# Two PSUM pools, single banks for the MLP, a later w1 load and an earlier first gate in a convolution and MLP block

## The chip, the cores and the metric

The kernel runs on one core of one Trainium2 chip. The metric is the device time of one execution in microseconds; the median of several runs is given, and beside it one profiled execution with its own time.

## The reference, cut to what matters

```python
def _A_ref(q, k, v, shift_k, ssm_k, ssm_D):            # S = 2048 tokens, D = 512
    k_shift = ...                                        # 4-tap causal shift filter of k
    kv = k_shift * v
    y = irfft(rfft(kv padded to 2S) * rfft(ssm_k padded to 2S))[:S]
    y = y + kv * ssm_D
    return q * y

def _B_ref(x, w1, w2):                                   # w1: 512 x 1376, w2: 1376 x 512
    return relu(x @ w1) @ w2

x = A_q
h = x + _A_ref(layernorm(x), A_k, A_v, A_shift_k, A_ssm_k, A_ssm_D)
out = h + _B_ref(layernorm(h), B_w1, B_w2)
```

The input and the output are bf16. The FFT stands for a causal convolution over 2048 tokens, of each of the 512 channels with its own filter.

## The kernel before

The instructions of each engine run in the order in which the code records them; the framework adds the semaphore waits. There is no planner that reorders anything. So the order on TensorE (PE), VectorE (DVE), ScalarE (ACT), GpSimd (POOL) and the DMA queue of SyncE (SP) is written out by hand in the source.

The work goes through these stages:

- **Filter and input, first stage (15 to 44 us).** `to_rows` (L278, L279) transposes the filter `sk` through PSUM into `kfl`. The loop over `u` in 0 to 7 then runs `s1(u)` (the first stage of the filter's transform, for one group of channels, with four "spike" matmuls at L293 that add `ssm_D` from `drow`) and `tap(u)` (the shift filter as matmuls at L329, times v at L332). The trigonometric tables are made in a scratch tile between them (`turns2`, L147 and L148; `sines2`, L142).
- **Second stage (44 to 72 us).** `second_k` finishes the filter's transform (L345, evicted at L266 or L268), `to_rows` brings the product `vT` into rows `xfl`, and `stage1_pairs` makes the first stage of the input's transform. In between, `column_means` (L365) forms the column means of w1 on TensorE, and `center` takes them off w1 on GpSimd: this is the second layer norm's mean, folded into w1.
- **Product (72 to 100 us).** `product(kp)` for 16 values of kp: second stage of the input, times the filter's transform.
- **Inverse (97 to 124 us).** 16 turns. Turn i has matmuls into `pi` (L486), a 32x32 transpose on VectorE (`inv_turn`, L491) and a rounding copy, on ScalarE for even i and GpSimd for odd i (`rounded`, L499 and L497). `last(q, d)` (L523) closes the inverse transform for tokens of quarter q and channel half d into `pz`. `last(0, 0)` needs blocks 0 to 7, `last(0, 1)` blocks 8 to 15.
- **Gate.** `gate(q, d)` multiplies `pz` by the normed input `qln` (L534), adds the input (L535) and sends the result `hp` through a transposing DMA into `hT` on SP's queue (L537). `ln1_norm` makes `qln`: on ScalarE for q = 0 (L513), on VectorE otherwise (L515). `norm1(q)` is statistics (L393, L395, and L397 and L398 on GpSimd) plus `ln1_norm`; `norm2(q)` is the statistics of `hp`.
- **MLP.** For each of the four sequence parts `sc` of 512 tokens, `mlp1(sc)` makes h1T = relu(w1^T hT) in 11 chunks of the 1376 columns (matmuls at L572, Relu on ScalarE at L608), and `mlp2(sc)` makes four token tiles (matmuls at L618, 11 in a group), each scaled and added to `hp` on VectorE (`o`, L623, two instructions a tile) and sent out (L627). For the first part `begin()` runs the half of four chunks that only needs `hT` of d = 0, ahead of the other half.

PSUM is one pool `ps` of four tiles, each of two banks of 512 f32, and `bank2(name)` takes the next tile in turn, whatever it is for. In `mlp1` two chunks fill the two banks of a tile, and one Relu of 128x1024 reads both. In `mlp2` two token tiles share a tile, and `o` reads one bank at a time.

The weights w1 are loaded by `load_w1()`: four DMAs of 344 KB on SP's queue (L125), into the same memory slot (tag "w") that the scratch tile held. So they wait until nothing reads the scratch tile any more. It is called after `sines2(1, 1, ...)` at u = 2. w2 is loaded by ScalarE's queue after the first transposes of the MLP (L595, L597).

The order of the MLP's pieces at the end:

```python
norm1(1)
mlp1(0)
norm2(0)
last(1, 0)
gate(1, 0, mp)
last(1, 1)
gate(1, 1, mp)
norm1(2)
mlp2(0)
last(2, 0)
...
```

Of the kernel before, what the change touches and what calls it, by code (L numbers as in the profile page):

```python
# [11 lines left out]
F32 = mybir.dt.float32  # L12
# [43 lines left out]
def kernel(  # L56
# [29 lines left out]
    tabp = pl.push("tabp", side="right")  # L86
    rows = pl.push("rows", side="right")
    early = pl.push("early", side="right")
    psum = pl.push("ps", bufs=4, space=PSUM)


    sk = rows.tile([P, DC, S], BF16, tag="r", name="sk")
    nc.sync.dma_start(out=sk[:], in_=A_ssm_k.rearrange("(c p) t -> p c t", p=P))
    wsh = consts.tile([P, DC, KS], BF16, name="wsh")
    nc.scalar.dma_start(out=wsh[:], in_=A_shift_k.rearrange("(r p) j -> p r j", p=P))
    drow = consts.tile([P, 64], BF16, name="drow")
    nc.gpsimd.memset(drow[:], 0.0)
# [17 lines left out]


    w1 = None
    scratch = w1p.tile([P, 2, 16, 64], I32, tag="w", name="scratch")
# [39 lines left out]
    r2 = scratch[:, 0]  # L158
# [49 lines left out]
    nc.gpsimd.memset(ones[:], 1.0 / D)  # L208

    def turns2(i, b):  # L210
        ta = scratch[:, 1]
        _turns(ta, r2, n2c[:], 8192, o2[:, i, b:b + 1])
        return ta

# [52 lines left out]
        else:  # L267
            nc.vector.tensor_copy(out=o, in_=i)  # L268

    def bank2(name):  # L270
        return psum.tile([P, 2, 512], F32, tag="ps", name=name)


    def to_rows(src, q, fl):
# [127 lines left out]
    for u in range(8):  # L402
        s1(u)
        if u == 1:
            sines2(1, 0, turns2(1, 0))
        if u == 2:
            sines2(1, 1, turns2(1, 1))
            load_w1()
            negated(2)
            negated(3)  # L410
        if u == 4:
            inverse_tables()
        tap(u)
    pl.pop("early")
    xfl = rows.tile([P, 64, 2, 64], BF16, tag="r", name="xfl")

# [90 lines left out]
    def ln1_norm(q, pool, tiles=range(4)):  # L507
        if 0 in tiles:
            qn[q] = pool.tile([P, 4, D], BF16, tag="qln", name="qln", bufs=2 if q else 1)
        for i in tiles:  # L510
            t = 4 * q + i
            if q == 0:
                nc.scalar.activation(out=qn[q][:, i, :], in_=xh[q][:, i, :], func=ACT.Identity, scale=rstd1[:, t, :], bias=nmr[:, i:i + 1])  # L513
            else:
                nc.vector.tensor_scalar(out=qn[q][:, i, :], in0=xh[q][:, i, :], scalar1=mv1[:, t, 0:1],  # L515
                                        scalar2=rstd1[:, t, :], op0=ALU.subtract, op1=ALU.mult)

    def last(q, d):
        pz = bank2("pz")[:].rearrange("p b (i c) -> p (b i) c", c=256)
        pzs[q, d] = pz  # L520
        for i in range(4):
            for t in range(2):
                nc.tensor.matmul(out=pz[:, i, :], lhsT=tf[:, 4 * q + i, t:t + 2].rearrange("p t a n -> p (t a n)"),  # L523
                                 rhs=a1x[:, d, 16 * t + 4 * q + i, :], start=(t == 0), stop=(t == 1))

    def gate(q, d, pool, parts=(slice(0, 4),)):
        if d == 0:
            hp[q] = pool.tile([P, 2, 4, 256], BF16, tag="hp", name="hp", bufs=3 if q else 1)
            hT[q] = pool.tile([P, 2, 4, 2, P], BF16, tag="hT", name="hT", bufs=2 if q else 1)
        part = lambda t: t.rearrange("p i (r d g) -> p i r d g", r=DC, d=2)[:, :, :, d]  # L530
        h = hp[q][:, d]
        for ts in parts:
            hr = h[:, ts].rearrange("p i (r g) -> p i r g", r=DC)
            nc.vector.tensor_tensor(out=hr, in0=pzs[q, d][:, ts].rearrange("p i (r g) -> p i r g", r=DC), in1=part(qn[q][:, ts]), op=ALU.mult)  # L534
            nc.vector.tensor_tensor(out=hr, in0=hr, in1=part(xh[q][:, ts]), op=ALU.add)  # L535
        if (q, d) != (0, 1):
            nc.sync.dma_start_transpose(out=hT[q][:, d].rearrange("p i r t -> p (i r) t"), in_=h.rearrange("p i c -> p (i c)"))  # L537

    blocks = []
    spots = [(i // 8, 32 * (i % 8)) for i in range(16)]  # L540
    tiles = [bank2("pi") for _ in range(2)]
    for b in range(2):
        for i in range(2):
            inv_half(tiles[i], *spots[i], b)
    for i in range(16):
        if i >= 2:
            tiles.append(bank2("pi"))
            for b in range(2):
                inv_half(tiles[i], *spots[i], b)
        blocks.append(inv_turn(tiles[i], *spots[i]))  # L550
        if i < 14:
            rounded("AP"[i % 2], blocks[i])
        if i in (4, 6):
            ln1_norm(0, late, range(i - 4, i - 2))
        if i == 10:
            last(0, 0)
        if i == 11:
            gate(0, 0, late)

    for i in (14, 15):  # L560
# [8 lines left out]
    def first(sc, ps1, fc, cs):  # L569
        fsz = min(P, DFF - fc * P)  # L570
        for c in cs:
            nc.tensor.matmul(out=ps1[:fsz, fc % 2, :].rearrange("p (i t) -> p i t", i=4), lhsT=w1[:, c, fc * P:fc * P + fsz],  # L572
                             rhs=hT[sc][:, c // 2, :, c % 2, :], start=(c == 0), stop=(c == DC - 1))
# [11 lines left out]
    pst = bank2("pst")[:].bitcast(BF16)[:, 0, :].rearrange("p (i t) -> p i t", t=P)  # L585
    for i in range(8):
        nc.tensor.transpose(out=pst[:, i, :], in_=hp[0][:, 1, i // 2, P * (i % 2):P * (i % 2) + P], identity=ident[:])
        if i % 4 == 3:
            nc.scalar.copy(out=hT[0][:, 1].rearrange("p i r t -> p (i r) t")[:, i - 3:i + 1], in_=pst[:, i - 3:i + 1])
    pl.pop("mid")  # L590
    pl.pop("a1kp")
    mp = pl.push("mp", side="right")
# [5 lines left out]
    def mlp1(sc):  # L598
        h1T = mp.tile([P, NFC, 512], BF16, tag="h1T", name="h1T", bufs=2)
        h1s[sc] = h1T  # L600
        for f0 in range(0, NFC, 2):
            fcs = range(f0, min(f0 + 2, NFC))
            early = sc == 0 and f0 // 2 < len(begun)
            ps1 = begun[f0 // 2] if early else bank2("ps1m")
            for fc in fcs:
                first(sc, ps1, fc, (2, 3) if early else range(DC))
            fsz = min(P, DFF - f0 * P)
            nc.scalar.activation(out=h1T[:fsz, f0:f0 + len(fcs), :], in_=ps1[:fsz, 0:len(fcs), :], func=ACT.Relu)  # L608

    def mlp2(sc):  # L610
        h1T = h1s[sc]
        for j in range(2):
            ps2 = bank2("ps2m")
            for i in range(2 * j, 2 * j + 2):
                t = 4 * sc + i
                for fc in range(NFC):
                    ksz = min(P, DFF - fc * P)
                    nc.tensor.matmul(out=ps2[:, i % 2, :], lhsT=h1T[:ksz, fc, i * P:(i + 1) * P], rhs=w2[:ksz, fc, :],  # L618
                                     start=(fc == 0), stop=(fc == NFC - 1))
                o = mp.tile([P, D], BF16, tag="o", name="o", bufs=4)  # L620
                for d in range(2):
                    half = lambda a: a.rearrange("p (r d g) -> p d r g", r=DC, d=2)[:, d]
                    nc.vector.scalar_tensor_tensor(out=half(o[:]), in0=half(ps2[:, i % 2, :]), scalar=rstd2[:, t, :],  # L623
                                                   in1=hp[sc][:, d, i, :].rearrange("p (r g) -> p r g", r=DC),
                                                   op0=ALU.mult, op1=ALU.add)
# [36 lines left out]
    mlp2(3)  # L662
    pl.close_all()

# [29 lines left out]
```

## Time and profile before

| what | value |
|---|---|
| three runs | 241.17 us median, 238.05 to 243.74 |
| the profiled execution | 238.82 us, with a span of 237.0 us from its first to its last instruction |
| TensorE busy | 180.9 us, 76% of the span |
| VectorE busy | 150.1 us, 63% |
| ScalarE busy | 95.3 us, 40% |
| GpSimd busy | 92.1 us, 39% |
| chain that ended last, by engine | PE 52%, DVE 19%, issue 9%, POOL 8%, DMA 5%, ACT 4% |
| mean granted TensorE clock | 0.949 |

The profile gives times in microseconds from the start of the span and durations of one instruction in nanoseconds. PE is the matmul part of TensorE, PEld its weight loads, L572 is line 572 of the kernel. A matmul's end is modelled, so consecutive matmuls overlap in the records. "Issue" is time in which an engine waited for nothing that the profile shows. The granted clock is the share of full clock that TensorE had; it changes between 0.50 and 1.00.

### The profile page before, as it was taken

Reading aid. Unit: us, or ns where it says so; the run is one execution under the profiler, and the core shown is the slowest. Engines: PE = TensorE matmul, PEld = TensorE weight load, DVE = VectorE, ACT = ScalarE, POOL = GpSimd, SP = SyncE. Lnnn points to the kernel's source line nnn. Section 1 sums busy time; section 2 is a strip of 40 time slices with the busy share of each in tenths; the row PEclk is TensorE's granted clock in tenths of the full one; section 3 lists DMA queues with packets and bytes.
Section 4 is the critical chain, followed back from the end, with each engine's and each line's share of the span. In section 5 each row is a group of like instructions: output and inputs, shape, how many; then the busy total and the mean of one; then the engine's idle time right before and its main releaser. Section 6 shows DMA issues by size and latency. Waiting matters only on the chain.

```text
span 237.0 us, 4368 instructions
## 1 busy us (share of the span) xinstructions
PE 180.9 (76%) x1804; PEld 112.5 (47%) x1816; DVE 150.1 (63%) x225; ACT 95.3 (40%) x95; POOL 92.1 (39%) x111
## 2 busy tenths in 40 slices
PE   0489776998986777696947990989909899889883
PEld 0475443687765667474624450344503445334331
DVE  4777984497966999999877767246371372343121
ACT  3214853457799343179772620005400044006300
POOL 7889980008931999858650222002020020002000
PEclk9999999799999999999967996799976999999999
DMA  6999994000000000094020613013021130320011
GB/s 210 280 234 182 188 218 98 3 4 0 3 3 3 1 0 3 0 239 118 0 44 6 232 21 71 22 46 66 0 44 25 46 66 0 66 47 22 0 44 44
DMA packets 31331, 16.00 MB, mean 67 GB/s; under 512 B 26224, under 2 KB 29648, under 8 KB 31312
## 3 DMA queue, kind: packets, MB, share of 16 engines
q1 hardware_dynamic: 28976, 14.05, 27.9%
q10 hardware_dynamic: 2336, 1.68, 2.5%
q8 instruction: 14, 0.23, 0.4%
q14 instruction: 5, 0.04, 0.1%
HBM read 7.54 MB, written 2.10 MB: 41 GB/s over the span
## 4 chain that ended last, share of the span: by engine, by line
PE 52%; DVE 19%; issue 9%; POOL 8%; DMA 5%; ACT 4%; DVEq 0%; SPq 0%; POOLq 0%
PE ps1m L572 16%; PE ps2m L618 13%; POOL a1k L468 6%; DVE zs L491 5%; PE pkv L329 4%; PE pst L278 4%; DMA sk<-in_A_ssm_k_dram 3%; PE pz L523 3%; DVE o L623 3%; PE ps2k L345 3%; PE ps L316 2%; PE pi L486 2%; DVE st L393 2%; DMA out_dram<-o 2%; DVE a1k L268 2%
## 5 line engine op out<-in xcount | busy, mean ns | idle before, releaser
L618 PE MATMUL ps2m<-w,h1T 128*128 128x512 bf16 (+1 forms) x172 | 43.1, 402 | 18.9 <-DVE o L623 18.7
L608 ACT ACTIVATE h1T<-ps1m 128x1024 bf16<-128x1024 f32 (+1 forms) x24 | 22.3, 950 | 70.2 <-PE ps1m L572 70.2
L572 PE MATMUL ps1m<-hT,w 128*128 128x512 bf16 (+1 forms) x176 | 40.8, 391 | 4.1 <-DMA hT<-hp 3.4
L397 POOL TENSOR_SCALAR rstd<-mv 128x4 f32<-128x4 f32 x8 | 1.8, 228 | 103.0 <-DVE mv L395 103.0
L623 DVE SCALAR_TENSOR_TENSOR o<-ps2m,rstd,hp 128x256 bf16<-128x256 f32 x32 | 14.0, 480 | 39.2 <-PE ps2m L618 39.2
L618 PEld LDWEIGHTS <-h1T 128*128 128x128 bf16 (+1 forms) x176 | 17.7, 102 | 42.8 <-issue 25.6
L572 PEld LDWEIGHTS <-w 128*128 128x128 bf16 (+1 forms) x176 | 17.6, 102 | 24.8 <-DMA hT<-hp 3.8
L468 POOL TENSOR_TENSOR a1k<-usb,a1k 128x1024 fp32r<-128x1024 f32 x10 | 23.7, 2398 | 8.9 <-DVE a1x L463 8.9
L345 PE MATMUL u<-a1x,tab 64*128 64x256 f32 x256 | 18.9, 290 | 7.7 <-ACT usb L462 4.0
L345 PEld LDWEIGHTS u<-a1x,tab 64*128 64x128 f32 x256 | 16.3, 184 | 10.2 <-ACT usb L462 5.3
L499 ACT CAST a1x<-zs 128x1024 fp32r<-128x1024 f32 (+2 forms) x10 | 17.0, 1721 | 9.2 <-DVE zs L491 9.2
L534 DVE TENSOR_TENSOR hp<-pz,qln 128x1024 bf16<-128x1024 f32 (+1 forms) x9 | 9.9, 1100 | 17.0 <-PE pz L523 16.8
L463 DVE TENSOR_TENSOR a1x<-u,a1k 128x1024 fp32r<-128x1024 f32 x16 | 18.7, 1216 | 2.2 <-PE u L345 2.2
L491 DVE STREAM_TRANSPOSE zs<-pi 128x1024 f32<-128x1024 f32 x16 | 18.4, 1216 | 1.5 <-POOL a1x L497 1.1
L497 POOL CAST a1x<-zs 128x1024 fp32r<-128x1024 f32 (+1 forms) x8 | 15.8, 1978 | 8.5 <-DVE zs L491 8.5
L266 ACT CAST a1k<-ps 128x1024 fp32r<-128x1024 f32 x12 | 11.7, 1011 | 12.9 <-PE ps L300 12.9
L329 PE MATMUL pkv<-kT,wdiag 128*128 128x512 bf16 x56 | 15.7, 401 | 0.6
L462 ACT COPY usb<-u 128x1024 f32<-128x1024 f32 x10 | 10.0, 1012 | 11.1 <-POOL a1k L468 11.1
L486 PE MATMUL pi<-a1k,wd 128*128 128x512 f32 x32 | 13.3, 416 | 1.2 <-POOL a1k L468 1.1
L332 DVE TENSOR_TENSOR vT<-pkv,vT 128x1024 bf16<-128x1024 f32 x8 | 9.8, 1220 | 6.0 <-PE pkv L329 6.0
L278 PE MATMUL pst<-identw,sk 128*128 128x128 f32 x32 | 6.5, 394 | 9.1 <-DMA sk<-in_A_ssm_k_dram 9.1
L266 ACT CAST a1k<-ps2k 128x1024 fp32r<-128x1024 f32 x11 | 10.6, 1018 | 6.4 <-PE ps2k L345 6.4
(102 smaller groups left out, 286.6 us busy)
## 6 DMA issues: line engine op xcount, KB each, us to landing
sk<-in_A_ssm_k_dram SPq DMA_DIRECT2D x1, 2048.0 KB, 8.2
xall<-in_A_q_dram SPq DMA_DIRECT2D x16, 128.0 KB, 3.4
out_dram<-o SPq DMA_DIRECT2D x56, 32.0 KB, 1.6
w<-in_B_w_dram SPq DMA_DIRECT2D x4, 344.0 KB
w<-in_B_w_dram ACTq DMA_DIRECT2D x1, 1280.0 KB, 6.1
x<-in_A_q_dram SPq DMA_DIRECT2D x4, 128.0 KB, 3.2
out_dram<-o ACTq DMA_DIRECT2D x8, 32.0 KB, 1.7
hT<-hp SPq DMA_TRANSPOSE x7, 3.1
```

What stands on the lines that cost most here:

```text
L266: nc.scalar.copy(out=o, in_=i)
L329: nc.tensor.matmul(out=ps[:, i, :], lhsT=wdiag[:, 2 * h + i, j, :], rhs=kT[c][:, 2 * h + i, 16 - j:CH + 16 - j], start=(j == 0), stop=(j = ...
L345: nc.tensor.matmul(out=ps[:, d, 256 * i:256 * i + 256], lhsT=tab[rw, k1, b:b + 2, :].rearrange("p b k -> p (b k)"), rhs=a_in[rw, c, k1, :] ...
L463: nc.vector.tensor_tensor(out=spot(a1x, kp), in0=u2[:], in1=kk.bitcast(F32), op=ALU.mult)
L468: (nc.gpsimd if pool else nc.vector).tensor_tensor(out=kk, in0=(usb if pool else u1)[:], in1=kk.bitcast(F32), op=ALU.mult)
L486: nc.tensor.matmul(out=ps[:, b, :], lhsT=wd[:, m:m + 2, :].rearrange("p b k -> p (b k)"), rhs=src[:, d, 16 * b:16 * b + 16, c0:c0 + 32], s ...
L491: nc.vector.transpose(out=zs[:], in_=ps[:].rearrange("p b (k c) -> p c (b k)", c=32))
L499: nc.scalar.copy(out=o, in_=i)
L572: nc.tensor.matmul(out=ps1[:fsz, fc % 2, :].rearrange("p (i t) -> p i t", i=4), lhsT=w1[:, c, fc * P:fc * P + fsz], rhs=hT[sc][:, c // 2, ...
L608: nc.scalar.activation(out=h1T[:fsz, f0:f0 + len(fcs), :], in_=ps1[:fsz, 0:len(fcs), :], func=ACT.Relu)
L618: nc.tensor.matmul(out=ps2[:, i % 2, :], lhsT=h1T[:ksz, fc, i * P:(i + 1) * P], rhs=w2[:ksz, fc, :], start=(fc == 0), stop=(fc == NFC - 1))
L623: nc.vector.scalar_tensor_tensor(out=half(o[:]), in0=half(ps2[:, i % 2, :]), scalar=rstd2[:, t, :], in1=hp[sc][:, d, i, :].rearrange("p (r ...
```

## The change

- The PSUM pool becomes two pools, `psA` and `psB`, of two tiles each. `bank2` takes them in turn, or from the pool that it is told.
- From the MLP on, `last` and the transposes `pst` use pool 0. The MLP takes both tiles of pool 1 once (`m2`), and `bank()` hands out their four single banks in turn. Each chunk of `mlp1` and each token tile of `mlp2` has one bank; a Relu now reads 128x512.
- `pst` writes its two halves into two banks.
- `drow` becomes a part of the scratch tile, and `load_w1()` is called after the loop over u, since the spike matmuls of u = 7 are then the last readers of the slot.
- The first gate is recorded at turn 10 of the inverse, ahead of turn 11's transpose, and `ln1_norm` one turn sooner, after turns 3 and 5.
- The order of the MLP's pieces changes: `mlp1(0)` ahead of `norm1(1)`, `norm2(q)` behind a gate, both gates of quarter 2 ahead of `mlp1(1)`, both of quarter 3 ahead of `mlp1(2)`, `norm2(3)` behind `mlp1(3)`.

```diff
-    psum = pl.push("ps", bufs=4, space=PSUM)
+    psums = [pl.push(n, bufs=2, space=PSUM) for n in ("psA", "psB")]
+    turn = [0]
...
-    drow = consts.tile([P, 64], BF16, name="drow")
-    nc.gpsimd.memset(drow[:], 0.0)
+    scratch = w1p.tile([P, 2080], I32, tag="w", name="scratch")
+    drow = scratch[:, 2048:2080].bitcast(BF16)
+    nc.gpsimd.memset(drow, 0.0)
...
-    def bank2(name):
-        return psum.tile([P, 2, 512], F32, tag="ps", name=name)
+    def bank2(name, pool=None):
+        if pool is None:
+            pool = turn[0]
+            turn[0] = 1 - pool
+        return psums[pool].tile([P, 2, 512], F32, tag="ps", name=name)
...
             sines2(1, 1, turns2(1, 1))
-            load_w1()
             negated(2)
...
         tap(u)
+    load_w1()
...
-        pz = bank2("pz")[:].rearrange("p b (i c) -> p (b i) c", c=256)
+        pz = bank2("pz", 0 if (q, d) != (0, 0) else None)[:].rearrange("p b (i c) -> p (b i) c", c=256)
...
+    turn[0] = 0
     tiles = [bank2("pi") for _ in range(2)]
...
-        if i in (4, 6):
-            ln1_norm(0, late, range(i - 4, i - 2))
+        if i in (3, 5):
+            ln1_norm(0, late, range(i - 3, i - 1))
         if i == 10:
             last(0, 0)
-        if i == 11:
             gate(0, 0, late)
...
-            nc.tensor.matmul(out=ps1[:fsz, fc % 2, :].rearrange("p (i t) -> p i t", i=4), ...
+            nc.tensor.matmul(out=ps1[:fsz, :].rearrange("p (i t) -> p i t", i=4), ...
...
+    m2 = [bank2("m2", 1) for _ in range(2)]
+    used = [0]
+
+    def bank():
+        used[0] += 1
+        return m2[(used[0] - 1) // 2 % 2][:, (used[0] - 1) % 2, :]
...
     def begin():
-        begun.append(bank2("ps1m"))
         for i in range(2):
-            first(0, begun[-1], 2 * len(begun) - 2 + i, (0, 1))
+            begun.append(bank())
+            first(0, begun[-1], len(begun) - 1, (0, 1))
...
-        for f0 in range(0, NFC, 2):
-            fcs = range(f0, min(f0 + 2, NFC))
-            early = sc == 0 and f0 // 2 < len(begun)
-            ps1 = begun[f0 // 2] if early else bank2("ps1m")
-            for fc in fcs:
-                first(sc, ps1, fc, (2, 3) if early else range(DC))
-            fsz = min(P, DFF - f0 * P)
-            nc.scalar.activation(out=h1T[:fsz, f0:f0 + len(fcs), :], in_=ps1[:fsz, 0:len(fcs), :], func=ACT.Relu)
+        for fc in range(NFC):
+            fsz = min(P, DFF - fc * P)
+            early = sc == 0 and fc < len(begun)
+            ps1 = begun[fc] if early else bank()
+            first(sc, ps1, fc, (2, 3) if early else range(DC))
+            nc.scalar.activation(out=h1T[:fsz, fc, :], in_=ps1[:fsz, :], func=ACT.Relu)
...
-        for j in range(2):
-            ps2 = bank2("ps2m")
-            for i in range(2 * j, 2 * j + 2):
+        for i in range(4):
                 t = 4 * sc + i
+                ps2 = bank()
...
+    mlp1(0)
     norm1(1)
-    mlp1(0)
-    norm2(0)
     last(1, 0)
     gate(1, 0, mp)
+    norm2(0)
     last(1, 1)
     gate(1, 1, mp)
     norm1(2)
     mlp2(0)
     last(2, 0)
     gate(2, 0, mp)
+    last(2, 1)
+    gate(2, 1, mp)
     norm2(1)
     mlp1(1)
-    last(2, 1)
-    gate(2, 1, mp)
     norm1(3)
+    last(3, 0)
     mlp2(1)
-    last(3, 0)
     gate(3, 0, mp)
+    last(3, 1)
+    gate(3, 1, mp)
     norm2(2)
     mlp1(2)
-    last(3, 1)
-    gate(3, 1, mp)
     mlp2(2)
+    mlp1(3)
     norm2(3)
-    mlp1(3)
     mlp2(3)
```

More of the change, by code (lines that the diff above doesn't have):

```diff
@@ L117 @@
     w1 = None
-    scratch = w1p.tile([P, 2, 16, 64], I32, tag="w", name="scratch")
     def load_w1():
@@ L157 @@
         nc.gpsimd.iota(n2i[s:s + 64, :], pattern=[[0, 1]], base=0, channel_multiplier=1)
-    r2 = scratch[:, 0]
+    r2 = scratch[:, 0:1024].rearrange("p (a b) -> p a b", b=64)
     nc.gpsimd.iota(r2, pattern=[[2, 16], [128, 64]], base=1, channel_multiplier=0)
@@ L210, in turns2 @@
     def turns2(i, b):
-        ta = scratch[:, 1]
+        ta = scratch[:, 1024:2048].rearrange("p (a b) -> p a b", b=64)
         _turns(ta, r2, n2c[:], 8192, o2[:, i, b:b + 1])
@@ L571, in first @@
         for c in cs:
-            nc.tensor.matmul(out=ps1[:fsz, fc % 2, :].rearrange("p (i t) -> p i t", i=4), lhsT=w1[:, c, fc * P:fc * P + fsz],
+            nc.tensor.matmul(out=ps1[:fsz, :].rearrange("p (i t) -> p i t", i=4), lhsT=w1[:, c, fc * P:fc * P + fsz],
                              rhs=hT[sc][:, c // 2, :, c % 2, :], start=(c == 0), stop=(c == DC - 1))
+    m2 = [bank2("m2", 1) for _ in range(2)]
[3 more added lines that the diff above has]
+        return m2[(used[0] - 1) // 2 % 2][:, (used[0] - 1) % 2, :]
     def begin():
-        begun.append(bank2("ps1m"))
         for i in range(2):
-            first(0, begun[-1], 2 * len(begun) - 2 + i, (0, 1))
+            begun.append(bank())
+            first(0, begun[-1], len(begun) - 1, (0, 1))
     begin()
@@ L584 @@
     begin()
-    pst = bank2("pst")[:].bitcast(BF16)[:, 0, :].rearrange("p (i t) -> p i t", t=P)
+    pst = bank2("pst", 0)[:].bitcast(BF16)
     for i in range(8):
-        nc.tensor.transpose(out=pst[:, i, :], in_=hp[0][:, 1, i // 2, P * (i % 2):P * (i % 2) + P], identity=ident[:])
+        nc.tensor.transpose(out=pst[:, i // 4, P * (i % 4):P * (i % 4) + P], in_=hp[0][:, 1, i // 2, P * (i % 2):P * (i % 2) + P],
+                            identity=ident[:])
         if i % 4 == 3:
-            nc.scalar.copy(out=hT[0][:, 1].rearrange("p i r t -> p (i r) t")[:, i - 3:i + 1], in_=pst[:, i - 3:i + 1])
+            nc.scalar.copy(out=hT[0][:, 1].rearrange("p i r t -> p (i r) t")[:, i - 3:i + 1].rearrange("p i t -> p (i t)"),
+                           in_=pst[:, i // 4, 0:512])
     pl.pop("mid")
@@ L600, in mlp1 @@
         h1s[sc] = h1T
[L601 to L608 removed]
+        for fc in range(NFC):
[4 more added lines that the diff above has]
+            nc.scalar.activation(out=h1T[:fsz, fc, :], in_=ps1[:fsz, :], func=ACT.Relu)
     def mlp2(sc):
         h1T = h1s[sc]
[L612 to L614 removed]
+        for i in range(4):
                 t = 4 * sc + i
+                ps2 = bank()
                 for fc in range(NFC):
                     ksz = min(P, DFF - fc * P)
[L618 removed]
+                    nc.tensor.matmul(out=ps2, lhsT=h1T[:ksz, fc, i * P:(i + 1) * P], rhs=w2[:ksz, fc, :],
                                      start=(fc == 0), stop=(fc == NFC - 1))
@@ L622, in mlp2 @@
                     half = lambda a: a.rearrange("p (r d g) -> p d r g", r=DC, d=2)[:, d]
-                    nc.vector.scalar_tensor_tensor(out=half(o[:]), in0=half(ps2[:, i % 2, :]), scalar=rstd2[:, t, :],
+                    nc.vector.scalar_tensor_tensor(out=half(o[:]), in0=half(ps2), scalar=rstd2[:, t, :],
                                                    in1=hp[sc][:, d, i, :].rearrange("p (r g) -> p r g", r=DC),
```

## The prediction

> **What bounds the kernel now.** I read the page first (engine shares, the 40 slices), then TensorE's timeline through the inverse stage and the MLP, the groups by form, the chain that ended last around 39 us, and the busy windows there. The profiled execution took 238.82 us with a span of 237.0 us.
>
> ```profile
> PE 180.9 (76%) x1804; PEld 112.5 (47%) x1816; DVE 150.1 (63%) x225; ACT 95.3 (40%) x95; POOL 92.1 (39%) x111
> ...
> PE   0489776998986777696947990989909899889883
> ...
> PEclk9999999799999999999967996799976999999999
> ```
>
> From slice 22 (130 us) to the end TensorE carries the MLP, and what ends its waits there sets the time. Its timeline, with start, length and, in brackets, the idle time before a group and what ended it:
>
> ```profile
> 128.41 0.38 PE L587 MATMUL pst<-ident,hp 128*128 128x128 bf16 x4 [0.67 <-ACT hT L589]
> 129.47 7.93 PE L572 MATMUL ps1m<-hT,w 128*128 128x512 bf16 x36 [0.67 <-ACT hT L589]
> 137.05 2.25 PE L523 MATMUL pz<-a1x,tf 128*128 128x256 f32 x16
> 139.15 2.55 PE L618 MATMUL ps2m<-w,h1T 128*128 128x512 bf16 x10
> 148.56 6.29 PE L618 MATMUL ps2m<-w,h1T 128*128 128x512 bf16 x22 [6.86 <-DVE o L623]
> 155.81 2.54 PE L618 MATMUL ps2m<-w,h1T 128*128 128x512 bf16 x11 [0.97 <-DVE o L623]
> ...
> 203.31 4.92 PE L618 MATMUL ps2m<-w,h1T 128*128 128x512 bf16 x22 [1.02 <-DVE o L623]
> 209.19 2.54 PE L618 MATMUL ps2m<-w,h1T 128*128 128x512 bf16 x11 [0.97 <-DVE o L623]
> 211.56 9.66 PE L572 MATMUL ps1m<-hT,w 128*128 128x512 bf16 x44
> ```
>
> The reader is to see two things. The first product (L572) runs without a stop: 44 matmuls in 9.66 us, 0.216 us each, because both banks of a tile are filled before one Relu reads them. The second product (L618) stops before every second group of 11, for 0.97 to 1.02 us, until VectorE has read `o`. That group writes bank 1 of a tile, and VectorE was reading bank 0. So in this program a matmul waits for the last reader of the whole two-bank tile, not of its own bank. In the built change the wait is the same kind: the first matmul into `m2[...][:, 1]` waits for the Relu, or the `o`, that read bank 0 of that tile.
>
> **The MLP, part by part.** A recorded matmul lasts 0.38 us and the next starts 0.216 us after it, so a wait costs its idle time plus 0.164 us.
>
> `first` (L572) now fills one bank, and each bank is read by its own Relu. Of the 11 chunks of a sequence part, five go into bank 1 of the tile whose bank 0 was filled just before: five waits in each `mlp1`, 20 in all, and one more where `mlp2(2)` starts in bank 1 behind the last Relu. Each wait is one Relu of 128x512, which the trace does not hold. Its nearest rows:
>
> ```profile
> L608 ACT ACTIVATE h1T<-ps1m 128x1024 bf16<-128x1024 f32 x20 | 20.4, 1024 | 70.2 <-PE ps1m L572 70.2
> ...
> L608 ACT ACTIVATE h1T<-ps1m 96x512 bf16<-96x512 f32 x4 | 2.3, 583 | 0.0
> ...
> L589 ACT COPY hT<-pst 128x512 bf16<-128x512 bf16 x2 | 1.2, 586 | 3.3 <-PE pst L587 3.3
> ```
>
> I take 0.585 us; the same pattern stands in the timeline above, where a 586 ns copy kept TensorE idle for 0.67 us. So 21 x (0.67 + 0.164) = 17.5 us. Bounds: 0.67 alone, 14.1; the 0.97 idle of the VectorE waits, 23.8. The extra 20 Relus themselves lie on ScalarE, which is idle for 70.2 us before them.
>
> The `o` waits: before, eight. Now a pair sits in one tile once in `mlp2(0)`, twice in `mlp2(1)`, once in `mlp2(2)`, twice in `mlp2(3)`, and `mlp1(3)` starts in bank 1 behind the last `o` of `mlp2(2)`. Six of these seven are ordinary: 6 x (0.97 + 0.164) = 6.8 us. The seventh, in `mlp2(0)`, is long. `mlp1(0)` now ends at 129.47 + 36 x 0.216 + 5 x 0.834 + 0.1 (two Relus in a row) = 141.5. VectorE's `gate(1, 0)` needs the `pz` behind it, and `norm2(0)` now stands behind that gate instead of filling the time. VectorE's chain by its rows: gate at 141.5 + 1.13 = 142.6, then 1.86 + 2.72 (`norm2(0)`) + 1.86 + 5.51 (`norm1(2)`, statistics to the first `o`) = 154.6; the second `o` ends at 156.3. TensorE has done two groups by 141.5 + 2.0 + 22 x 0.216 = 148.3 and waits 8.0 us. After the long waits of before the granted clock fell to 0.50 (144.54 to 151.37), which cost 22 matmuls 1.4 us once (6.29 against 4.92) and 1.95 us once (6.87, at 178.10); I add 1.7.
>
> The second long wait of before (5.95 us at 178.1) goes: both gates, `norm2(1)` and `norm1(3)` take VectorE 13.7 us from 162, done by 176, and `mlp1(1)` with its own waits keeps TensorE busy until 178. The other gates that move lie beside TensorE's work in the same way; on SP's queue their transposing DMAs keep their places among the output DMAs.
>
> The sum from 129.47. Before: 344 matmuls x 0.216 = 74.3, six `pz` groups 6.0, waits 18.7 + 8 x 0.164 = 20.0, clock 3.3, together 103.6 (the trace has 103.4). After: 74.3 + 6.0 + 17.5 + 6.8 + 8.2 + 1.7 = 114.5. **The MLP loses 11 us**, by the bounds of the Relu wait 7.5 to 17.
>
> The Trainium skill's page Perfetto Trace Analysis (Optimizing Tensor Performance, Matmuls) says that independent groups should rotate through different banks so that one's eviction overlaps the next's matmuls. By that page four banks take all these waits away; what that gives here is the first rival. The 0.97 us rows above speak against it for two banks of one tile.
>
> **w1 behind the last first-stage group.** Four DMAs leave SP's queue at 39 us instead of 29.87; nothing is behind them there until `xall` at 99.80. What was beside them:
>
> ```profile
> 38.84 0.28 PE ps L300 x37
> 39.12 1.91 issue
> 41.03 0.38 PE ps L300 x27
> ...
> 42.00:48.00 6.00, 6.00 (x44) 4.28 (x43) 2.37 (x3) 3.03 (x4) 0.00 (x0) 0.72 0.01 3
> ```
>
> TensorE stood for 1.91 us with nothing to wait for but its own instructions, just as w1's traffic ended (the DMA share is 1.00 up to 38 us, 0.33 in the next). The idle time was followed by half clock from 42.15 to 45.56, another 3.41 x 0.5 = 1.7 us, while TensorE was busy without a break. If w1 held up the fetch, both go: 3.6 us. That is an inference; the lower bound is nothing. A similar stop of 1.50 us at 32.51 fell into the same traffic, with x0's beside it: 0 to 1.5, I take 0.4. Against it: `column_means(0)` (L365, at 50.07) needs all of w1. It would be reached at 46.5. w1's landing is bounded by w2's 6.1 us and by 9.0 us (29.87 to the end of its traffic at 38.9), so 45 to 48: a wait of 0 to 1.5, I take 0.8. **Net -3.2 us, bounds -5 to +1.5.** `drow` inside `scratch` costs nothing: the spike matmuls wait for the same producers as before.
>
> **The first gate.** VectorE idled 1.10 us before transpose 11, and the gate now goes there. But `ln1_norm` also moves ahead of blocks 4 and 6 on ScalarE: two 1.55 us pairs, 1.27 us later for block 6, whose cast then ends at 113.25 instead of 111.99, later than GpSimd's block 7 (112.04). So `pz` and transpose 10 start 1.2 us later. The gate ends 1.2 us sooner, its transposing DMA leaves at 117.1 instead of 118.32, and transpose 15 still ends at 122.9, which releases the next `pz`. **0 us**; bounds -1.5 (the half clock of 120.65 to 127.48 shrinks, since TensorE idles less before it) to +0.3. The two-pool split leaves the earlier stages' rotation over four tiles as it was: 0.
>
> **Sum:** 238.82 + 11.0 - 3.2 + 0 = 246.6 for an execution like the profiled one. That one lies 2.35 us under the median of the three runs (241.17, from 238.05 to 243.74); on the median the same change gives 249.0. I say **248.0**, between the two.
>
> **Rivals.** *Banks are free of each other* (the other side: faster). Place: the waits at the second bank of `m2`. If they follow the bank, the 21 Relu waits and all `o` waits but VectorE's own lag (0.4 us: with `mlp1(0)` unstopped the chain above starts 4.3 us sooner, and TensorE can do four groups before it needs the first `o`) vanish: 74.3 + 6.0 + 0.4 = 80.7, 22.7 less than before; with w1, about 213. It decides where each of the 21 waits costs less than 0.834 - 7.8/21 = 0.46 us. Against it: eight waits of before with VectorE reading the other bank. Chance 0.06.
>
> *w1 and clock give back most of it*: the full 5.0 and the 1.5 of the gate, and Relu waits at the lower bound: +7.5 - 6.5 = +1, 240 to 243. For it: the 1.91 us stop and the clock window. Chance 0.14.
>
> *w1 gives nothing*: the fetch stops for reasons of its own, or `column_means` takes the wait over: +11 to +12.5, 250 to 253. For it: DMA share was already 0.02 from 39 to 40 while TensorE still stood. Chance 0.19.
>
> *The clock falls in the stop-and-go product*: if half of the 168 matmuls of `first` ran at half clock, 84 x 0.216 = +18, about 266. Against it: TensorE would be busy 1.73 of every 2.56 us, and windows that granted half followed much less work (0.57 of 3.41 us from 141.13 to 144.54), while 60 to 70% busy slices held 9 on the page. Chance 0.05. The Trainium skill's page TensorE: Matmul & The Clock Gate (A second HAM failure mode: psum-queue depth-cycling) tells of such an oscillation between groups; no row here shows it.
>
> **How the numbers follow.** The forecast has 0.56. Faster by over 2%: 0.06. Within 2%: 0.14. Slower: 0.56 + 0.19 + 0.05 = 0.80. About 2% is what a measurement of this kernel can tell from no change. The range leaves out the first and last rivals: 242.0 to 254.0. The forecast's own part of it is 245 to 251.
>
> **What would show it.** In the profile after: 44 Relus of about 585 ns, and `first` with some 14 us idle ended by ACT `h1T`, in 20 places of about 0.67 us; one wait of about 8 us on `o` in `mlp2(0)` and none over 1.2 us later; no stop near 39 us, clock 1.00 through 42 to 48, and `column_means` at 47; the first hT transposing DMA 1.1 us earlier against the transposes. I am wrong if `first` shows no idle time by `h1T`, if the stop near 39 us stays, or if the granted clock is below 0.9 in `mlp1(2)`.

## The result, and the profile after

The changed kernel takes **250.75 us** (median of four runs, 249.93 to 252.03) against 240.48 for the kernel before (238.05 to 243.74): ratio 1.0467, 95% interval 1.0365 to 1.0569. It is slower. Times here are medians of all runs, while a ratio compares the means of those runs that lie within 1.5% of their kernel's fastest, so it can differ a little from the ratio of the medians. The profiled execution took 251.01 us, 12.2 us more than that of before.

From the page of the changed kernel, the engine row, the slices of TensorE and of its granted clock:

```profile
PE 185.3 (74%) x1804; PEld 112.6 (45%) x1816; DVE 149.5 (60%) x225; ACT 99.4 (40%) x115; POOL 92.0 (37%) x111
...
PE   0588999789777776949757870987788778867783
...
PEclk9999999999999999985977996599999999999999
```

TensorE has the same 1804 matmuls, ScalarE 20 more instructions, and where most of TensorE's slices held 9 in the MLP, most now hold 7 or 8, at full clock too. TensorE's timeline (start, length, and in brackets the idle time before a group and what ended it) shows how:

```profile
127.10 0.64 PE L577 MATMUL m<-hT,w 128*128 128x512 bf16 x2 [0.67 <-ACT hT L603]
128.42 1.86 PE L577 MATMUL m<-hT,w 128*128 128x512 bf16 x4 [0.69 <-ACT h1T L621]
130.97 2.72 PE L577 MATMUL m<-hT,w 128*128 128x512 bf16 x6 [0.69 <-ACT h1T L621]
134.37 1.89 PE L577 MATMUL m<-hT,w 128*128 128x512 bf16 x8 [0.69 <-ACT h1T L621]
136.94 1.89 PE L577 MATMUL m<-hT,w 128*128 128x512 bf16 x8 [0.69 <-ACT h1T L621]
139.52 1.89 PE L577 MATMUL m<-hT,w 128*128 128x512 bf16 x8 [0.69 <-ACT h1T L621]
141.05 2.26 PE L528 MATMUL pz<-a1x,tf 128*128 128x256 f32 x16
143.15 4.93 PE L630 MATMUL m<-w,h1T 128*128 128x512 bf16 x21
155.97 7.70 PE L630 MATMUL m<-w,h1T 128*128 128x512 bf16 x22 [7.89 <-DVE o L635]
```

`first` (now L577) stops five times in `mlp1(0)`, each time for 0.69 us until a Relu has read the other bank of its tile. `mlp2(0)` stops once, for 7.89 us, and its next 22 matmuls then take 7.70 us instead of 4.92. The groups give the sums (busy us and mean ns of one; then the idle time before them and what ended it):

```profile
L577 PE MATMUL m<-hT,w 128*128 128x512 bf16 (+1 forms) x176 | 44.4, 393 | 15.4 <-ACT h1T L621 13.8 <-DVE o L635 1.0 <-ACT hT L603 0.7
L630 PE MATMUL m<-w,h1T 128*128 128x512 bf16 (+1 forms) x172 | 41.9, 398 | 14.0 <-DVE o L635 13.0 <-ACT h1T L621 0.7
L621 ACT ACTIVATE h1T<-m 128x512 bf16<-128x512 f32 (+1 forms) x44 | 26.2, 597 | 80.6 <-PE m L577 80.6
```

VectorE's timeline shows why the long wait is long: it idles beside `mlp1(0)`, and only then come gate, `norm2(0)`, gate, `norm1(2)` and the first two tiles of `o`, in one row with no gap but 1.47 us for GpSimd. In this kernel the second and third token tiles share a tile of `m2`, so TensorE waits for the second `o`.

```profile
142.39 1.23 DVE L539 TENSOR_TENSOR hp<-pz,qln 128x1024 bf16<-128x1024 f32 x1 [10.89 <-PE pz L528]
...
144.26 2.47 DVE L398 BATCH_NORM_STATS2 st<-hp 128x6 f32<-128x512 bf16 x4
...
154.27 1.65 DVE L635 SCALAR_TENSOR_TENSOR o<-m,rstd,hp 128x256 bf16<-128x256 f32 x4
```

In the early stages the stop at 39 us is gone, and `column_means` (L370) waits for w1 instead, twice:

```profile
45.83 0.45 PE L370 MATMUL pm<-w,ones 128*128 128x344 bf16 x2 [0.64 <-DMA w<-in_B_w_dram]
47.05 1.05 PE L370 MATMUL pm<-w,ones 128*128 128x344 bf16 x6 [0.78 <-DMA w<-in_B_w_dram]
```

Between the two profiled executions, `mlp1(0)`'s second half starts 2.4 us earlier (127.10 against 129.47), and from there to the end of the last matmul the MLP takes 14.5 us longer (118.1 against 103.6).

### The profile page after: what moved, and what is told of

It reads as the page before. It is cut to its first block, busy times and chain, and to the rows that moved or that the text cites. A ratio compares the mean times of both kernels' runs of the same rounds, so it can differ in the third digit from the quotient of the medians.

```text
span 249.2 us, 4395 instructions
## 1 busy us (share of the span) xinstructions
PE 185.3 (74%) x1804; PEld 112.6 (45%) x1816; DVE 149.5 (60%) x225; ACT 99.4 (40%) x115; POOL 92.0 (37%) x111
## 4 chain that ended last, share of the span: by engine, by line
PE 46%; DVE 19%; ACT 14%; DMA 9%; issue 5%; SPq 3%; POOL 2%; DVEq 0%; POOLq 0%; ACTq 0%
PE m L577 17%; PE m L630 12%; ACT h1T L621 5%; DVE a1x L468 4%; DMA sk<-in_A_ssm_k_dram 3%; PE pst L283 3%; PE pkv L334 3%; PE pz L528 3%; DVE o L635 2%; DMA w<-in_B_w_dram 2%; PE ps L321 2%; DVE a1k L473 2%; DVE st L398 2%; ACT a1x L504 2%; DMA out_dram<-o 2%
## 5 line engine op out<-in xcount | busy, mean ns | idle before, releaser
L621 ACT ACTIVATE h1T<-m 128x512 bf16<-128x512 f32 (+1 forms) x44 | 26.2, 597 | 80.6 <-PE m L577 80.6
L577 PE MATMUL m<-hT,w 128*128 128x512 bf16 (+1 forms) x176 | 44.4, 393 | 15.4 <-ACT h1T L621 13.8
L630 PE MATMUL m<-w,h1T 128*128 128x512 bf16 (+1 forms) x172 | 41.9, 398 | 14.0 <-DVE o L635 13.0
L635 DVE SCALAR_TENSOR_TENSOR o<-m,rstd,hp 128x256 bf16<-128x256 f32 x32 | 13.9, 479 | 56.8 <-PE m L630 47.6
L577 PEld LDWEIGHTS <-w 128*128 128x128 bf16 (+1 forms) x176 | 17.6, 102 | 40.4 <-issue 24.3
L350 PE MATMUL u<-a1x,tab 64*128 64x256 f32 x256 | 19.8, 291 | 6.9 <-DVE a1x L468 2.6
L491 PE MATMUL pi<-a1k,wd 128*128 128x512 f32 x32 | 14.4, 450 | 2.0 <-DVE a1k L471 1.1
L334 PE MATMUL pkv<-kT,wdiag 128*128 128x512 bf16 x56 | 14.8, 381 | 0.6
L528 PE MATMUL pz<-a1x,tf 128*128 128x256 f32 x64 | 10.4, 314 | 5.0 <-ACT a1x L504 5.0
L491 PE MATMUL pi<-a1x,wd 128*128 128x512 f32 x32 | 13.7, 429 | 0.0
```

What stands on the lines that cost most here:

```text
L334: nc.tensor.matmul(out=ps[:, i, :], lhsT=wdiag[:, 2 * h + i, j, :], rhs=kT[c][:, 2 * h + i, 16 - j:CH + 16 - j], start=(j == 0), stop=(j = ...
L350: nc.tensor.matmul(out=ps[:, d, 256 * i:256 * i + 256], lhsT=tab[rw, k1, b:b + 2, :].rearrange("p b k -> p (b k)"), rhs=a_in[rw, c, k1, :] ...
L491: nc.tensor.matmul(out=ps[:, b, :], lhsT=wd[:, m:m + 2, :].rearrange("p b k -> p (b k)"), rhs=src[:, d, 16 * b:16 * b + 16, c0:c0 + 32], s ...
L577: nc.tensor.matmul(out=ps1[:fsz, :].rearrange("p (i t) -> p i t", i=4), lhsT=w1[:, c, fc * P:fc * P + fsz], rhs=hT[sc][:, c // 2, :, c % 2 ...
L621: nc.scalar.activation(out=h1T[:fsz, fc, :], in_=ps1[:fsz, :], func=ACT.Relu)
L630: nc.tensor.matmul(out=ps2, lhsT=h1T[:ksz, fc, i * P:(i + 1) * P], rhs=w2[:ksz, fc, :], start=(fc == 0), stop=(fc == NFC - 1))
```

## The experiments

The theory was: a matmul waits for the last reader of the whole tile in which it writes, whichever bank that reader used, so two consecutive pieces of work in one two-bank tile run one after the other. The rivals: the bank pair or the shorter Relu costs the time whatever the tile; VectorE's lag is the real bound; the order of the pieces makes the loss. Ratios are to the kernel before, timed beside each experiment; its median was 238.1 to 240.5 us there, so times of two experiments that weren't timed together can be off against each other by some 2 us.

### Four one-bank tiles

```diff
-    m2 = [bank2("m2", 1) for _ in range(2)]
-    used = [0]
+    pl.pop("psB")
+    psM = pl.push("psM", bufs=4, space=PSUM)
     def bank():
-        used[0] += 1
-        return m2[(used[0] - 1) // 2 % 2][:, (used[0] - 1) % 2, :]
+        return psM.tile([P, 512], F32, tag="m", name="m")[:]
```

> The changed kernel, but the four banks of the MLP are four tiles of one bank each instead of halves of two tiles; the banks, the order of the work and every instruction's size stay. Theory A (the program's waits are kept per tile, so a matmul into one bank waits for the reader of the other bank of its tile): all waits of `first` for h1T go (21 x 0.85 = 17.9 us), the six ordinary waits for `o` (6.8), the long one (8.2) and the half clock behind it (2.8), 35.7 us in all: about 215 us, and 215 to 222 if VectorE's or a DMA's lag takes a part of it over; no idle time of `first` ended by ACT h1T above a few tenths. Rival B (the wait comes with writing one bank while an engine reads the other bank, or with the shorter Relu, whatever the tile): the 0.69 us waits stay, 249 to 252. Rival C (the waits were a matter of the tile, but VectorE's chain of gate, statistics and `o` is the bound right behind): 226 to 235, with long waits for DVE o.

**215.71 us** (213.43 to 217.34; before 239.09), ratio 0.8981 (0.89 to 0.9062). The groups and TensorE's timeline from `mlp1(0)`'s second half:

```profile
L620 ACT ACTIVATE h1T<-m 128x512 bf16<-128x512 f32 (+1 forms) x44 | 26.2, 597 | 47.5 <-PE m L577 47.5
L577 PE MATMUL m<-hT,w 128*128 128x512 bf16 (+1 forms) x176 | 40.7, 391 | 1.8 <-DVE zs L496 0.7
L629 PE MATMUL m<-w,h1T 128*128 128x512 bf16 (+1 forms) x176 | 38.7, 379 | 0.0
```

```profile
126.24 9.62 PE L577 MATMUL m<-hT,w 128*128 128x512 bf16 x36 [0.67 <-ACT hT L602]
135.51 2.26 PE L528 MATMUL pz<-a1x,tf 128*128 128x256 f32 x16
137.61 9.69 PE L629 MATMUL m<-w,h1T 128*128 128x512 bf16 x44
146.94 2.26 PE L528 MATMUL pz<-a1x,tf 128*128 128x256 f32 x16
149.64 9.67 PE L577 MATMUL m<-hT,w 128*128 128x512 bf16 x44 [0.43 <-DVE o L634]
```

The same 44 Relus of 597 ns and the same order of work, and from `mlp1(0)`'s second half on no wait is left but one of 0.43 us. 250.75 - 215.71 = 35.0 us; the waits and the half clock behind them had been put at 35.7. So neither the shorter Relu nor the bank pair costs the time, and VectorE's lag was no bound of its own: with four tiles TensorE may run four groups ahead of the first `o`.

### The two tiles taken in turn

```diff
-        return m2[(used[0] - 1) // 2 % 2][:, (used[0] - 1) % 2, :]
+        return m2[(used[0] - 1) % 2][:, (used[0] - 1) // 2 % 2, :]
```

> The changed kernel, but its two m2 tiles are taken in turn (bank 0 of one, bank 0 of the other, bank 1 of one, ...), so a matmul into a bank follows the reader of that tile's other bank by two pieces of work instead of one. Theory A: a chunk of `first` waits for the Relu two chunks back, which has had 4 x 0.216 = 0.86 us for 0.69 + 0.16 = 0.85 us: the 21 waits shrink from 0.69 to 0 to 0.1 us, the six ordinary waits for `o` go, the long one in mlp2(0) stays at 6 to 8 us, since its third group still needs the first `o`: 250.7 - 17.9 - 6.8 = 226, 224 to 230. Rival B (bank pair or Relu itself): 249 to 252.

**223.98 us** (223.74 to 225.06; before 239.09), ratio 0.9408 (0.9341 to 0.9475).

```profile
129.51 1.08 PE L577 MATMUL m<-hT,w 128*128 128x512 bf16 x4 [0.26 <-ACT h1T L621]
130.78 6.20 PE L577 MATMUL m<-hT,w 128*128 128x512 bf16 x28 [0.20 <-ACT h1T L621]
136.64 2.25 PE L528 MATMUL pz<-a1x,tf 128*128 128x256 f32 x16
138.73 4.93 PE L630 MATMUL m<-w,h1T 128*128 128x512 bf16 x22
150.77 6.40 PE L630 MATMUL m<-w,h1T 128*128 128x512 bf16 x22 [7.11 <-DVE o L635]
```

The tiles are still two banks wide; only a piece of work now lies between two uses of one tile. The 0.69 us waits go but for two of 0.26 and 0.20 us, and so do all ordinary `o` waits: 26.8 us less than the changed kernel, where 24.7 was expected. What this version has and the four tiles lack is the long wait: the third group of `mlp2(0)` needs the first `o`. That and the half clock behind it, 7.11 + 1.48 = 8.6, account for the 8.3 us between the two.

### The wider Relu back in the changed kernel

```diff
-        for fc in range(NFC):
...
-            ps1 = begun[fc] if early else bank()
-            first(sc, ps1, fc, (2, 3) if early else range(DC))
-            nc.scalar.activation(out=h1T[:fsz, fc, :], in_=ps1[:fsz, :], func=ACT.Relu)
+        for f0 in range(0, NFC, 2):
+            fcs = range(f0, min(f0 + 2, NFC))
...
+            ps1 = m2[f0 // 2 % 2]
+            for fc in fcs:
+                first(sc, ps1[:, fc % 2, :], fc, (2, 3) if early else range(DC))
...
+            nc.scalar.activation(out=h1T[:fsz, f0:f0 + len(fcs), :], in_=ps1[:fsz, 0:len(fcs), :], func=ACT.Relu)
+        used[0] = 0
```

> The changed kernel, but mlp1 fills both banks of an m2 tile before one Relu of 128x1024 reads them, as in the kernel before; mlp2 keeps one bank for a token tile, and each part starts it in bank 0. Theory A: the 21 Relu waits go (17.9 us); there are eight waits for `o` instead of seven (+1.1), and the long one in mlp2(0) comes one group of 2.4 us earlier and lasts that much longer: 250.7 - 17.9 + 1.1 + 2.4 = 236, 234 to 238. Rival (the Relu waits are not worth what they last, because the lag behind them is VectorE's): 242 to 248.

**236.38 us** (233.85 to 237.47; before 238.14), ratio 0.9897 (0.9784 to 1.001). This takes out the largest term by itself. Against the changed kernel it is 14.4 us by medians. To that come what this version waits more: the long wait, 9.48 us instead of 7.89 (1.6), one more ordinary wait for `o` (1.2) and two waits of 0.25 us for the Relu ahead of `mlp2` (0.8). Together that is 18.0 us, and the 21 Relu waits, idle time and 0.164 us each, had been put at 17.9. The two kernels weren't timed together, so this agrees within some 2 us and no closer.

```profile
128.68 9.62 PE L577 MATMUL m<-hT,w 128*128 128x512 bf16 x36 [0.67 <-ACT hT L603]
137.94 2.26 PE L528 MATMUL pz<-a1x,tf 128*128 128x256 f32 x16
140.05 2.55 PE L633 MATMUL m<-w,h1T 128*128 128x512 bf16 x10
152.08 7.04 PE L633 MATMUL m<-w,h1T 128*128 128x512 bf16 x22 [9.48 <-DVE o L638]
```

### Tiles in turn in the second product of the kernel before

```diff
+        two = [bank2("ps2m") for _ in range(2)]
         for j in range(2):
-            ps2 = bank2("ps2m")
             for i in range(2 * j, 2 * j + 2):
+                ps2 = two[i % 2]
...
-                    nc.tensor.matmul(out=ps2[:, i % 2, :], ...
+                    nc.tensor.matmul(out=ps2[:, i // 2, :], ...
...
-                    nc.vector.scalar_tensor_tensor(out=half(o[:]), in0=half(ps2[:, i % 2, :]), ...
+                    nc.vector.scalar_tensor_tensor(out=half(o[:]), in0=half(ps2[:, i // 2, :]), ...
```

> The kernel before, with the two PSUM tiles of each mlp2 taken in turn by its four token tiles (the first and third share a tile, the second and fourth) and nothing else. Theory A (waits are kept per tile): the kernel before paid for this already; its six ordinary waits for `o` go (6 x 1.13 = 6.8 us) and each long one shrinks by the group of 2.4 us that TensorE may do first: 11.6 us in all, about 227 us, 225 to 230. Rival B (bank pair): 238 to 241.

**227.10 us** (224.66 to 232.34; before 239.60), ratio 0.9554 (0.9434 to 0.9674). The kernel before paid for the same thing: its ordinary waits for `o` are gone, and the long ones last 4.48 and 3.57 us instead of 6.86 and 5.95.

```profile
138.31 4.93 PE L619 MATMUL ps2m<-w,h1T 128*128 128x512 bf16 x21
147.72 6.31 PE L619 MATMUL ps2m<-w,h1T 128*128 128x512 bf16 x22 [4.48 <-DVE o L624]
...
191.62 9.69 PE L619 MATMUL ps2m<-w,h1T 128*128 128x512 bf16 x43
```

### The new order in the kernel before

The edit is the last part of the diff, the order of the MLP's pieces, and nothing else.

> The kernel before with the new order of the MLP's pieces and nothing else. Theory: the first long wait for `o` grows by norm2(0) that now stands behind gate(1,0) (2.7 us), the second long one (5.95 us, with 1.95 us of half clock behind it) becomes an ordinary one: -4.3 us in all, 236 to 238. Rival: the order costs more than it gives, because VectorE's idle time ahead of gate(1,0) isn't used: 241 to 244. If the single banks and not the order are the cause of the loss, this run is not slower than before by 2%.

**234.22 us** (231.28 to 235.56; before 239.09), ratio 0.9787 (0.9696 to 0.9879): a gain of about 4.9 us by medians, where 4.3 was expected (the time itself lies below the 236 to 238 that had been named). `norm2(0)` behind the gate makes the first long wait longer, 9.49 us instead of 6.86, and the second is an ordinary one:

```profile
151.92 6.61 PE L618 MATMUL ps2m<-w,h1T 128*128 128x512 bf16 x22 [9.49 <-DVE o L623]
...
177.78 4.92 PE L618 MATMUL ps2m<-w,h1T 128*128 128x512 bf16 x22 [0.97 <-DVE o L623]
```

### The order of before in the changed kernel

> The changed kernel with the order of the MLP's pieces of before. Theory: the Relu waits (21 x 0.85) stay, the long wait in mlp2(0) shrinks by norm2(0) (2.7 us), and a second long wait in mlp2(1) of 3 to 6 us with half clock behind it comes back: 249 to 255, still slower than before by over 3%. Rival C (the order makes the loss): 238 to 244.

**252.68 us** (251.99 to 256.13; before 239.09), ratio 1.0594 (1.0523 to 1.0664).

```profile
152.22 6.54 PE L630 MATMUL m<-w,h1T 128*128 128x512 bf16 x22 [5.26 <-DVE o L635]
...
182.89 6.56 PE L630 MATMUL m<-w,h1T 128*128 128x512 bf16 x22 [5.95 <-DVE o L635]
```

The first long wait is 2.63 us shorter (`norm2(0)` takes 2.72), the second comes back. With the new order the ratio is 1.0467, with that of before 1.0594: the order made none of the loss, and rather helped.

### The later w1 load alone

The edit is `drow` in the scratch tile and `load_w1()` behind the loop over u, in the kernel before.

> The kernel before with the later w1 load alone (drow inside the scratch tile, the load after the loop over u). Theory (w1's traffic held up TensorE's own instructions): the stop of 1.91 us at 39 us and the half clock from 42.15 to 45.56 go, column_means comes at about 47 us instead of 50.07, and the end moves by 1.9 to 2.9 us, as it did between the two profiled executions up to the inverse stage: ratio 0.988 to 0.992. Rival 1 (the stop has reasons of its own): it stays, ratio 1.00. Rival 2 (the stages behind pace themselves on VectorE and GpSimd and give it back): column_means comes 3 us earlier and the MLP less than 1 us earlier, ratio 0.997 to 1.003.

**238.44 us** (236.51 to 241.21, 12 runs) against 239.60 for before (234.20 to 243.83, 23 runs). By the ratio, 1.0096 (1.0023 to 1.017), it is 1% slower; by the means of all runs, 238.65 and 238.76, it is 0.1 us faster, with two standard errors of 1.3. Neither shows a gain, and the expected 1.9 to 2.9 us are not there. In its trace the stop at 39 us is gone, and w1 is waited for:

```profile
46.49 0.45 PE L365 MATMUL pm<-w,ones 128*128 128x344 bf16 x2 [0.49 <-DMA w<-in_B_w_dram]
47.91 1.05 PE L365 MATMUL pm<-w,ones 128*128 128x344 bf16 x6 [0.97 <-DMA w<-in_B_w_dram]
```

### w1 loaded early with four one-bank tiles

The edit against the kernel with four one-bank tiles:

```diff
-    drow = scratch[:, 2048:2080].bitcast(BF16)
-    nc.gpsimd.memset(drow, 0.0)
+    drow = consts.tile([P, 64], BF16, name="drow")
+    nc.gpsimd.memset(drow[:], 0.0)
...
             sines2(1, 1, turns2(1, 1))
+            load_w1()
...
-    load_w1()
     pl.pop("early")
```

> The changed kernel with four one-bank tiles for the MLP (215.7 us against 239.1 for the kernel before), but with w1 loaded early as in the kernel before. Theory (w1's traffic): 1.9 to 2.9 us slower than with the late load, ratio to the kernel before 0.906 to 0.910. Rival: the stages in between take it back, ratio 0.898 as with the late load.

**216.52 us** (213.00 to 219.36; before 239.60), ratio 0.9061 (0.8923 to 0.9199), against 215.71 with the late load: 0.8 us, less than either spread. Also not resolved.

What the times can't settle, the traces of all twelve kernels help with, since they fall into two sets. In the five with the early load TensorE stops near 39 us for 1.91, 2.18, 1.91, 1.64 and 1.36 us; in none of the seven with the late load. So the stop comes with w1's early load (`drow` changes its place with it each time). The traces also record the 16 KB packets of a queue that they call instruction (q8). After one that starts near 31 us (30.15 to 31.71) the next starts at 33.87 to 35.40 us in the seven, and only at 37.35 to 38.66 in the five, when w1's traffic runs out; TensorE goes on 1.2 to 1.7 us after that packet has landed. This bears out the forecast's inference that the load held up the fetch of instructions, in time though not as a shown cause, since no record says whose instructions they are.

But in all seven `column_means` waits for w1, 1.46 us on average in its two waits. It ends at 48.8 us on average with the late load and at 50.0 with the early one, 49.6 without the profiled execution of before. **The move is worth about 1 us at that point**, of which the end shows nothing that can be told from the spread.

### The first gate alone

```diff
-        if i in (4, 6):
-            ln1_norm(0, late, range(i - 4, i - 2))
+        if i in (3, 5):
+            ln1_norm(0, late, range(i - 3, i - 1))
         if i == 10:
             last(0, 0)
-        if i == 11:
             gate(0, 0, late)
```

> The kernel before with the first gate at turn 10 and ln1_norm one turn sooner, nothing else. Theory: the first transposing DMA of hT leaves about 1 us sooner against the transposes, block 6's rounding copy and pz come 1 us later, the last transpose of the inverse stays: 0 to -0.5 us, ratio 0.997 to 1.001. Rival (the half clock of 120.65 to 127.48 goes with the shorter idle time): -1.5 us, ratio 0.994.

**238.26 us** (235.49 to 241.58, 12 runs), ratio 1.0056 (0.9988 to 1.0124); the means differ by 0.7 us, with two standard errors of 1.4. No difference is resolved. Its trace shows a wait that changes its place. TensorE at the end of the inverse, first in the kernel before, then here:

```profile
121.46 1.89 PE L572 MATMUL ps1m<-hT,w 128*128 128x512 bf16 x4 [3.40 <-DMA hT<-hp]
123.66 2.05 PE L523 MATMUL pz<-a1x,tf 128*128 128x256 f32 x8 [0.31 <-ACT a1x L499]
```

```profile
119.30 1.04 PE L571 MATMUL ps1m<-hT,w 128*128 128x512 bf16 x4
122.64 1.18 PE L523 MATMUL pz<-a1x,tf 128*128 128x256 f32 x8 [2.30 <-ACT a1x L499]
```

The 3.40 us wait for the transposing DMA is gone, and TensorE waits 2.30 us for the rounding copy of the last block, which `pz` needs.

### norm2(0) beside mlp1(0), with four one-bank tiles

The edit against the kernel with four one-bank tiles:

```diff
     norm1(1)
+    norm2(0)
     last(1, 0)
     gate(1, 0, mp)
-    norm2(0)
```

> The changed kernel with four one-bank tiles for the MLP, and norm2(0) put ahead of last(1, 0), into the 6.2 us in which VectorE idles beside mlp1(0). Theory: TensorE's waits in the MLP are down to 0.43 us there, so what VectorE does sooner is worth 0 to 0.4 us: 215 to 216, ratio to the kernel before 0.89 to 0.905. Rival: the first parts of the MLP still wait for VectorE in places that the timeline merges into groups: 213 to 214.

**214.18 us** (213.77 to 214.36; before 238.14), ratio 0.8997 (0.8936 to 0.9058), against 0.8981 (0.89 to 0.9062) without the move: the same. The time lies between the two ranges that had been named, nearer to the rival's, but the ratio doesn't bear the rival out. The order on VectorE, worth 2.6 us in the long wait of the changed kernel, is worth nothing where TensorE doesn't wait for VectorE. This version and the first experiment's beat the kernel before by a tenth and the changed one by a seventh.

## Why the prediction was right

The forecast was 248.0 us and slower, and the mechanism of its main part, the waits kept per tile, is the one that the runs show. That its number came within 2.75 us is in part luck. By its steps:

- **The Relu waits (17.5 us): right.** 20 waits of about 0.69 us in `first` (13.8 in all) and one of 0.68 in `mlp2(2)`, instead of 0.67 each. Removing them alone gave what they add up to, within what the two timings allow.
- **The ordinary `o` waits and the long one: right.** The long wait is 7.89 us (forecast 8.0), none later is over 1.12, and VectorE's chain from the gate to the first `o` takes 11.9 us (142.39 to 154.27; forecast 12.0). That the chain also starts where it was forecast (142.6) is luck: `mlp1(0)`'s second half began 2.4 us earlier than in the kernel before, on whose times the forecast was worked out, and half clock stretched it by 2.1.
- **The MLP's sum (+11.0): too small, by 3.5 us, and the failed terms are those of the clock.** The half clock behind the long wait lasted 10.24 us (151.41 to 161.65) and cost the 22 matmuls 2.8 us (7.70 - 4.92), where 1.7 was added from the two cases of before. And a half clock of 6.83 us (127.52 to 134.34) fell on `mlp1(0)`: its groups of 4 and 6 matmuls there take 1.86 and 2.72 us, where 8 take 1.89 behind them, some 2.1 us in all. In the execution of before the half clock at this place had ended (at 127.48) before `mlp1(0)`'s second half began. With 0.02 more for each Relu wait: 1.1 + 2.1 + 0.4 = 3.6. The stretch behind the long wait (length, busy time of PE, PEld, DVE, ACT and POOL with their instructions, granted clock, DMA share, GB/s):

```profile
151.40:161.70 10.30, 5.73 (x14) 2.02 (x14) 3.89 (x12) 0.00 (x0) 1.26 (x2) 0.50 0.11 26
```

- **w1 (-3.2): wrong in two terms.** The stop went, as forecast. But the wait at `column_means`, taken as 0.8, is 1.46, at its upper bound; and the half clock of 42.15 to 45.56 (1.7 us) did not follow from the stop alone: of the five traces with the stop only that of before has it. The trace of the gate's experiment has the same stop (2.18 us), and the same stretch at full clock. The same window of busy times in the kernel before, then there (the column behind POOL's is the granted clock):

```profile
42.15:45.56 3.41, 3.41 (x18) 1.88 (x17) 1.81 (x2) 0.44 (x2) 0.00 (x0) 0.50 0.02 5
```

```profile
42.15:45.56 3.41, 3.41 (x33) 2.38 (x33) 2.13 (x2) 1.88 (x3) 0.00 (x0) 1.00 0.02 5
```

  TensorE is busy throughout in both, with 18 matmuls or 33. With the means of the two sets: 1.80 for the stop and 0.65 for the one at 32.5 us, less 1.46, is 1.0 us. Since the profiled execution of before happened to have that half clock, `column_means` ends 3.25 us earlier in the trace after than in it, which looks like the forecast -3.2, but the kernels don't differ by that.
- **The gate (0): nothing in the runs against it.** The mechanism was the one given: the DMA leaves sooner, the rounding copy and `pz` come later.
- **The sum.** Both errors have the same sign: between the two profiled executions the MLP lost 3.5 us more than forecast, and the stages ahead of it gave 2.4 us instead of 3.2. So the sum of the terms, 246.6, is 4.4 us under the profiled 251.01. The median of the changed kernel is only 2.75 us above the stated 248.0 because 1.4 us had been added there for the spread of the kernel before; the changed kernel's profiled execution lies at its median, so this allowance hid a part of the error. The rival in which w1 gives nothing (250 to 253) describes the w1 part of the result better than the forecast did.
- **The rival in which banks are free of each other** had the right price (213 against 215.7 and 214.2 measured) for a kernel whose banks are tiles of their own. The chip lets them be free; it is this program's waits, kept per tile, that didn't. The Trainium skill's page Perfetto Trace Analysis (Optimizing Tensor Performance, Matmuls) asks for groups that rotate through banks; the 0.0 us of idle time in the second product with four one-bank tiles agrees with it, once each bank is a tile.

## What to carry to other kernels

Where waits are kept per tile, splitting a tile into banks that are used one after the other buys no overlap and adds a wait at every second bank; a tile for each bank, or another tile's work between two uses, does. Before a wait is costed, ask how many pieces of work lie between two uses of the same tile, and whether the reader needs longer than these. And a half clock seen in one profiled execution is no term of a sum until a second execution shows it at the same place.

## What the runs showed of the hardware

**Every long wait for `o` was followed by half clock.** In the traces of all kernels here TensorE waited 14 times for `o` for 3.57 to 9.49 us, and each time the 22 matmuls behind it took 6.29 to 7.86 us instead of 4.92: 1.4 to 2.9 us more, after the shortest wait (1.67) as after longer ones. Behind waits of 1.12 us and less, 0.69 us in every 2.57 among them, the changed kernel ran at full clock from 161.65 us to the end. Half clock also came without such a wait, as from 42.15 us in the kernel before. It lasted 3.41, 6.83 or 10.24 us, whole steps of 3.41. The Trainium skill's page TensorE: Matmul & The Clock Gate (Part 1: The HAM clock gate) gives a window of 3413 ns that runs on by itself, and the steps agree with it. Which stretch is hit depends on where the windows fall; that is our reading of it, not shown by a run.

**The spread of the kernel before goes in part with this clock.** Over its 37 runs beside the experiments (234.20 to 243.83 us) the half-clock time, worked out as twice the missing clock share times the span, goes from 17 to 34 us, in groups near 17, 21, 24 and 27.5 with one run each at 31 and 34. A straight line through them gives 0.45 us for each us of it, with a correlation of 0.73, which leaves about half of the variance to other causes; at half clock a busy TensorE loses 0.5.
